# Attention in sub-blocks of 64 positions instead of blocks of 128, ahead of two MLPs

## The chip, the cores and the metric

The kernel runs on one core of a Trainium2 chip. The metric is the device time of one execution in microseconds (us). The times before are 577.37 us (median of three runs, 576.85 to 577.47).

## The reference

A gated linear attention runs over 4 sequences of 768 positions with 8 heads; its output goes through two MLPs of width 256 to 2048 to 256. The attention is written in chunks of 32 positions, but its result does not depend on the chunk: a kernel may take any length, as long as it hands the state on.

```python
for c in range(nc):
    cum = np.cumsum(la, axis=-1)
    L = np.exp(cum[:, :, :, None] - cum[:, :, None, :]) * causal
    M = np.einsum('bhin,bhjn->bhij', Cc, Bc) * L
    y_intra = np.einsum('bhij,bhjd->bhid', M, xc)
    y_inter = np.einsum('bhin,bhnd->bhid', Cc, state) * np.exp(cum)[:, :, :, None]
    y[:, :, sl] = y_intra + y_inter
    Bx = np.einsum('bhjn,bhjd->bhjnd', Bc, xc) * decay_from_j[:, :, :, None, None]
    state = decay_full[:, :, None, None] * state + np.sum(Bx, axis=2)
x = softplus(x @ w_in) @ w_out              # first MLP
g = np.where(h >= 1, h, np.where(h <= -1, 0, (h + 1) ** 2 / 4))   # second MLP, h = x @ w2_in
return g @ w2_out
```

## The kernel before

The 768 positions are cut into six blocks (c = 0 to 5) of Q = 128. A unit u is one block of one sequence, so there are 24 units; from the second block on, two sequences of a block are worked on as a pair. The first MLP takes a block's 512 columns as soon as its four units are done, and its matmuls fill TensorE between the attention's.

`program()` lists the work as jobs with an engine, a cost, what they need and which buffers they take. A planner (`Jobs.order`) turns the list into one fixed order for each engine, and `tile_kernel` emits it. So a changed cost or need moves instructions far from the code that changed. Each engine works its list strictly in order; a job that waits holds back all that stands behind it.

For a pair from the second block on, the jobs are: `rows` (a transfer that copies a unit's clipped decays to all 128 partitions), `decay` (one VectorE scan a unit, L915, that turns them into the matrix of decays, 128 positions by 8 heads by 128), `scores` (TensorE, L951, the products of C and B), `weigh` (VectorE, L960, scores times decays, two a unit), `cd` (L935, C times the running decay), `sources` (L923, B times the decay to the block's end), and `out` (TensorE): the part from the old state (L986), the part within the block (L993), and in the same PSUM tile the block's own sum for the next state (L1000; not in the last block). Then `evac` copies the output from PSUM (ScalarE, L1019), `ready` subtracts for its low half (VectorE, L1027) and updates the state (L1030), and `sm` spreads the state for the next block's `out` (ScalarE, L1038). There is one pair of PSUM banks, `y`, which `scores` and `out` share in turn; `ready` gives it back.

These matmuls have plain 32-bit operands; each is recorded as two passes, and each pass as a weight load and a matmul. They use a part of the array each (32 or 128 rows by 32, 64 or 128 columns), and those on different parts run side by side. The MLP's matmuls (L1061 to L1063, L1197) use the whole array.

Of the kernel before, what the change touches and what calls it, by code (L numbers as in the profile page):

```python
# [15 lines left out]
Q = 128  # L16
NC = S // Q
NU = NC * NB
# [171 lines left out]

def ready_of(u):

    return u if u < NB else u | 1
# [7 lines left out]
def program():  # L201
# [39 lines left out]
    for u in range(NU):  # L241
# [4 lines left out]
        if c == 0:  # L246
            for hg in range(2):
                add(
                    ("spread", u, hg), PE, 470, needs=[("columns", hg), ("rows_of", u)] + ([("spread", u, 0)] if hg else []),
                    takes=[("acc", "h")] + ["ld"] * (hg == 0),  # L250
                )
                add(("decay", u, hg), ACT, 520, needs=[("spread", u, hg)], gives=[("part", ("spread", u, hg), 0)])
            decay = [("decay", u, 0), ("decay", u, 1)]
        else:
            add(("rows", u), SP, 400, needs=["store"], takes=["ld"], size=524e3)
            add(("decay", u), DVE, 2220, needs=[("rows", u)])
            decay = [("decay", u)]
            add(("cd", u), DVE, 200, needs=[("load", u), ("dec", c)])
# [6 lines left out]
        elif c < NC - 1:  # L265
            add(("sources", u), DVE, 210, needs=[("load", u)] + decay, takes=["bt"])
        if b % 2:
            v = u // 2
            add(
                ("scores", v), PE, 1270, needs=[("load_bc", v)] + (decay + [("decay", u - 1)] if c else [("scores", v - 1)] * v),  # L270
# [3 lines left out]
        for hg in range(2):  # L274
            n = 2 * u + hg
            weighed = [("decay", u, hg), ("sources", u, hg)] if c == 0 else decay + [("sources", u)] * (c < NC - 1)
# [6 lines left out]
            else:  # L283
                add(("weigh", u, hg), DVE, 600, needs=weighed + [("weigh", u, 0)] * hg + [("scores", u // 2)], gives=bank)
        both = [u] if c == 0 else [u - 1, u]
        if c == 0 or b % 2:

            needs = [("weigh", i, hg) for i in both for hg in range(2)] + ([("out", both[0] - 1)] if u else [])
            if c > 0:
                needs += [(kind, i - NB * (kind == "sm")) for i in both for kind in ("cd", "sm")]  # L290
            add(
                ("out", u), PE, 2200 if c else 750, needs=needs, takes=["y"],
                gives=[("load", i) for i in both] + [("rows", i) if c else ("part", ("spread", u, 0), 1) for i in both]
                + [("sources", i) if c else ("sources", u, 0) for i in both] * (c < NC - 1),
# [5 lines left out]
            if c == 1:  # L300
# [5 lines left out]
                ("ready", u), DVE, 610 + 380 * (c < NC - 1) if c else 340, due=due, needs=[("evac", u)],  # L306
                gives=[("out", u)] + [("dec", c)] * (b == NB - 1 and c > 0),
            )
        if c < NC - 1:
            add(("sm", u), ACT, 500, needs=[("ready", ready_of(u))] + [("decay", 3, 1)] * (u < NB))  # L310
# [165 lines left out]
DEC_DMAS = 1  # L476
# [10 lines left out]
def tile_kernel(ctx: ExitStack, tc: tile.TileContext, a0, al, bc, ub, w_in, w_out, w2_in, w2_out, out):  # L487
# [48 lines left out]
    s_t = [base.tile([128, 64], F32, name=f"s{b}") for b in range(NB - 1)]  # L536
# [5 lines left out]
    base.tile([128, 244], F32, name="pad")  # L542
# [6 lines left out]
    eye_t = base.tile([128, H * Q], F32, tag="eye0", name="eye_t")  # L549
    sm_t = [base.tile([128, 64], F32, name=f"sm{b}") for b in range(NB)]  # L550
    s_t.append(base.tile([128, 64], F32, name="s3"))
    idle, eye16, later = (base.tile([128, Q], BF16, name=n) for n in ("idle", "eye16", "later"))

    more = [base.tile([128, 512], F32, tag=f"more{i}", name=f"more{i}") for i in range(1)]
# [6 lines left out]
    def home(tag):  # L561

        if tag not in homes:
            n = {"ld": 1024, "st": 1024, "eye": 1024, "bc": 768}.get(tag[:-1], 512)
# [7 lines left out]
    units = [(f"u{i}", 0) for i in range(4)] + [("eye0", 0), ("eye0", 1), ("dec0", 0), ("dec1", 0), ("more0", 0)]  # L572
# [7 lines left out]
    def plain(tag, part):  # L580

        key = tag + " plain"
        if key not in homes:
            n = {"st": 1024, "eye": 1024}.get(tag[:-1], 512)
# [20 lines left out]
    clip_z = dram.tile([NU, H * Q], F32, name="clip_z")  # L605
    clip_p = dram.tile([NC * 2, 4, NB, Q], F32, name="clip_p")
# [178 lines left out]
    heads, z_t = (flat(buf("dec", i)).rearrange("p (h i) -> p h i", h=4)[0:nr] for i in range(2))  # L785
# [51 lines left out]
    @job  # L837
    def clip_load(engine):
        tiles["clip"] = new(of("clip_load"), F32, "clip0").rearrange("p (h i) -> p h i", h=4)[0:nr]
        nc.sync.dma_start(tiles["clip"], al.rearrange("r (h i) -> r h i", h=4))  # L840
# [9 lines left out]
    def store(engine, *step):  # L850
# [5 lines left out]
        else:  # L856
            nc.sync.dma_start(clip_z.rearrange("u (g h i) -> (u g) h i", g=2, i=Q), z_t)
# [30 lines left out]
    def rows(engine, u):  # L888
# [3 lines left out]
        nc.sync.dma_start(flat(ld_t(u)), clip_z[r:r + 1].to_broadcast([128, H * Q]))  # L892

    @job
    def dec(engine, c):
        t = mine("dec", c)[0]
        src = clip_p.rearrange("(c g) h b i -> c (g h) (b i)", g=2)[c]
        nc.sync.dma_start(flat(t), src.unsqueeze(1).to_broadcast([H, N, NB * Q]))

    def ld_t(u):  # L900
        return buf(*got["rows", u][0]) if u >= NB else buf(*got["spread", u, 0][1])
# [18 lines left out]
    def sources(engine, u, hg=None):  # L920
# [4 lines left out]
            in1=ld_t(u)[:, h, Q - 1:Q].to_broadcast([128, h.stop - h.start, N]), op=ALU.mult,  # L925
# [6 lines left out]
    def cd(engine, u):  # L932

        t = parts(u)[2]
        nc.vector.tensor_tensor(out=t, in0=t, in1=mine("dec", u // NB)[0][:, u % NB, :], op=ALU.mult)  # L935
# [21 lines left out]
    def weigh(engine, u, hg):  # L957
        ld = flat(ld_t(u)[:, 4 * hg:4 * hg + 4])
        if engine == DVE:
            nc.vector.tensor_tensor(out=ld, in0=cb_t(u, hg), in1=ld, op=ALU.mult)  # L960
# [14 lines left out]

    def out_unit(engine, u):
        c, b = divmod(u, NB)
        units = [u] if c == 0 else [u - 1, u]

        if c > 0:  # L980
            for i in units:
                y, cdt = y_t(i)[0], parts(i)[2]
                for p in range(4):

                    r, o = slice(p * 32, p * 32 + 32), p % 2 * 64
                    nc.tensor.matmul(  # L986
                        y[o:o + 64, p // 2], sm_t[i % NB][r], cdt[r], start=(i == units[0]), stop=False, skip_group_check=True,
                    )
        for i in units:
            y, x, ld = y_t(i)[0], parts(i)[0], ld_t(i)  # L990
            for h in range(H):
                r = slice(h % 4 * 32, h % 4 * 32 + 32)
                nc.tensor.matmul(  # L993
                    y[r, h // 4], x[:, h * 32:h * 32 + 32], ld[:, h, :], start=(c == 0), stop=True, skip_group_check=True,
                )
        for i in units if c < NC - 1 else []:
            state, x, bt = y_t(i)[1], parts(i)[0], flat(bt_t(i))
            for p in range(4):
# [4 lines left out]
                )  # L1003

# [9 lines left out]
    def evac(engine, u):  # L1014
# [5 lines left out]
        if c == 0:  # L1020
            nc.scalar.copy(s_t[b], y_t(u)[1])

    @job
    def ready(engine, u):
# [3 lines left out]
        for i in (u - 1, u) if 0 < c < NC - 1 else ():  # L1028
            s = s_t[i % NB]
            nc.vector.scalar_tensor_tensor(  # L1030
                out=s, in0=s, scalar=mine("dec", c)[0][:, i % NB, Q - 1:Q], in1=y_t(i)[1], op0=ALU.mult, op1=ALU.add,
            )

    @job
    def sm(engine, u):
        b = u % NB
        for e in range(2):
            nc.scalar.activation(  # L1038
                out=sm_t[b][:, e * D:(e + 1) * D], in_=s_t[b][:, e * D:(e + 1) * D], func=AF.Copy, scale=of_one[:, e:e + 1],
            )  # L1040
# [183 lines left out]
    with tc.manual_schedule():  # L1224
# [3 lines left out]
        for i in range(WARM):  # L1228
# [4 lines left out]
        ones = buf("ld", 4)  # L1233
        nc.gpsimd.memset(ones[:, 0:2], 1.0)
        eye3 = eye_t.rearrange("p (h i) -> p h i", h=H)
        nc.gpsimd.affine_select(
            out=eye3[:, 0], in_=ones[:, 0], pattern=[[1, Q]],
# [8 lines left out]
        nc.vector.tensor_copy(eye16, eye3[:, 0])  # L1246
# [78 lines left out]
```

## Time and profile before

| | before |
|---|---|
| median of three runs | 577.37 us |
| profiled execution: time, span | 577.67 us, 576.0 us |
| TensorE busy | 563.8 us (98%) |
| VectorE busy | 461.2 us (80%) |
| ScalarE busy | 340.8 us (59%) |
| matmul passes | 3526 |

Busy times overlap, so they don't add up to the span. A matmul's recorded duration is longer than the time by which it holds up the next one: matmuls are pipelined, and what counts is the distance between their starts. The time that is not in the span (577.67 - 576.0 = 1.67 us) lies around it.

### The profile page before, as it was taken

How to read it: one execution, taken by the hardware profiler on the slowest of the kernel's cores; microseconds unless marked ns; L12 is line 12 of the kernel's file. 1: busy time of each engine (PE TensorE's matmuls, PEld its weight loads, DVE VectorE, ACT ScalarE, POOL GpSimd, SP SyncE). 2: the span in 40 equal slices, each digit the busy share in tenths (PEclk: the TensorE clock that was granted, in tenths of full speed). 3: DMA queues.
4: the chain of work that ended last, by engine and by line, in shares of the span. 5: the costliest groups of instructions: out<-in, count | busy, mean ns of one | idle time of the engine just before them, and what ended most of it. 6: DMA issues, size and time to landing. Idle time of an engine off the chain costs nothing.

```text
span 576.0 us, 9160 instructions
## 1 busy us (share of the span) xinstructions
PE 563.8 (98%) x3526; PEld 468.8 (81%) x3526; DVE 461.2 (80%) x777; ACT 340.8 (59%) x615; POOL 42.9 (7%) x42
## 2 busy tenths in 40 slices
PE   7799999999999999999999999999999999999997
PEld 3699989998877877888888788888887888788885
DVE  6899999968756684589999888987799776776674
ACT  5858554424414512666456777766677674777863
POOL 5211300000000340010000000200021000000000
PEclk9999999999999999999999999999999999999999
DMA  7976245514303200023431000000100001000001
GB/s 276 399 275 225 81 160 199 164 63 138 129 22 116 75 1 1 0 75 92 128 116 67 1 1 1 1 0 2 73 2 1 1 1 38 36 1 1 1 1 73
DMA packets 19863, 43.67 MB, mean 76 GB/s; under 512 B 1740, under 2 KB 2316, under 8 KB 19820
## 3 DMA queue, kind: packets, MB, share of 16 engines
q1 hardware_dynamic: 19820, 43.10, 22.0%
q8 instruction: 27, 0.44, 0.3%
q14 instruction: 16, 0.13, 0.1%
HBM read 39.75 MB, written 3.34 MB: 75 GB/s over the span
## 4 chain that ended last, share of the span: by engine, by line
PE 91%; DVE 5%; DMA 1%; issue 1%; ACT 1%; SPq 0%; DVEq 0%
PE acc L1197 42%; PE h L1061 6%; PE h L1063 6%; PE h L1062 6%; PE h L1068 3%; PE h L1070 3%; PE h L1069 3%; PE z L1068 3%; PE z L1070 3%; PE z L1069 3%; PE acc L1185 2%; PE y L951 2%; PE y L993 2%; PE z L1063 1%; PE z L1061 1%; PE z L1062 1%
## 5 line engine op out<-in xcount | busy, mean ns | idle before, releaser
L1171 DVE TENSOR_TENSOR gl<-g,gh 128x512 fp32r<-128x512 f32 x182 | 128.1, 706 | 36.3 <-PE acc L1197 22.2
L1197 PE MATMUL acc<-gh,woh 128*128 128x512 f32 (+1 forms) x424 | 152.3, 367 | 0.0
L1197 PE MATMUL acc<-gh,wol 128*128 128x512 f32 (+1 forms) x424 | 150.6, 363 | 0.0
L1197 PE MATMUL acc<-gl,woh 128*128 128x512 f32 (+1 forms) x424 | 115.5, 363 | 0.0
L1156 ACT ACTIVATE g<-h 128x512 f32<-128x512 f32 x74 | 44.2, 597 | 96.0 <-PE h L1063 88.9
L1197 PEld LDWEIGHTS acc<-gh,woh 128*128 128x128 f32 x424 | 79.8, 188 | 15.8 <-issue 1.7
L1197 PEld LDWEIGHTS acc<-gh,wol 128*128 128x128 f32 x424 | 79.9, 189 | 12.3
L611 ACT CAST gh<-g 128x512 fp32r<-128x512 f32 x110 | 68.2, 620 | 33.2 <-PE acc L1197 22.2
L1197 PEld LDWEIGHTS acc<-gl,woh 128*128 128x128 f32 x424 | 74.4, 189 | 12.7
L1061 PE MATMUL h<-xh,wih 128*128 128x256 f32 (+1 forms) x224 | 74.9, 334 | 0.0
L1062 PE MATMUL h<-xh,wil 128*128 128x256 f32 (+1 forms) x224 | 73.6, 328 | 0.0
L1063 PE MATMUL h<-xl,wih 128*128 128x256 f32 (+1 forms) x224 | 73.6, 328 | 0.0
L1148 ACT ACTIVATE t<-t 128x512 f32<-128x512 f32 x96 | 60.9, 634 | 2.2
L613 DVE CAST gh<-g 128x512 fp32r<-128x512 f32 x76 | 35.2, 467 | 26.6 <-ACT g L1156 22.4
L915 DVE TENSOR_TENSOR_SCAN ld<-ld,eye_t 128x1024 f32<-128x1024 f32 x20 | 47.3, 2367 | 1.9 <-DMA ld<-clip_z 1.9
L1061 PEld LDWEIGHTS h<-xh,wih 128*128 128x128 f32 x224 | 42.6, 190 | 4.6 <-issue 0.7
L1063 PEld LDWEIGHTS h<-xl,wih 128*128 128x128 f32 x224 | 42.5, 190 | 3.8
L1062 PEld LDWEIGHTS h<-xh,wil 128*128 128x128 f32 x224 | 42.6, 190 | 3.8
L1141 ACT ACTIVATE t<-h 128x512 f32<-128x512 f32 x37 | 22.1, 597 | 14.8 <-PE h L1070 11.5
L1141 ACT ACTIVATE t<-z 128x512 f32<-128x512 f32 x35 | 20.8, 595 | 9.7 <-PE z L1070 7.7
L1160 DVE TENSOR_TENSOR g<-h,t 128x512 f32<-128x512 f32 x37 | 25.4, 686 | 0.9 <-ACT t L1148 0.2
L1160 DVE TENSOR_TENSOR g<-z,t 128x512 f32<-128x512 f32 x35 | 23.9, 685 | 0.6
(335 smaller groups left out, 900.1 us busy)
## 6 DMA issues: line engine op xcount, KB each, us to landing
ld<-clip_z SPq DMA_DIRECT2D x20, 512.0 KB, 4.4
st<-in_w_in_dram SPq DMA_DIRECT2D x15, 512.0 KB, 4.0
st<-in_w_out_dram SPq DMA_DIRECT2D x15, 512.0 KB, 4.6
u<-in_ub_dram SPq DMA_DIRECT2D x24, 256.0 KB, 4.8
bc<-in_bc_dram SPq DMA_DIRECT2D x12, 384.0 KB, 6.1
out_dram<-st_plain SPq DMA_DIRECT2D x6, 256.0 KB, 2.2
dec<-clip_p SPq DMA_DIRECT2D x5, 256.0 KB
out_dram<-dec_plain SPq DMA_DIRECT2D x4, 256.0 KB
```

Source lines behind the costliest of these rows:

```text
L611: nc.scalar.copy(out, in_)
L613: engines[engine].tensor_copy(out, in_)
L915: nc.vector.tensor_tensor_scan(t, t, eye_t, 0.0, ALU.mult, ALU.add)
L1061: nc.tensor.matmul(o, wh, xh[c][:, k, t0:t0 + n], start=(k == 0), stop=False)
L1062: nc.tensor.matmul(o, wl, xh[c][:, k, t0:t0 + n], start=False, stop=False)
L1063: nc.tensor.matmul(o, wh, xl[c][:, k, t0:t0 + n], start=False, stop=(k == 1))
L1141: nc.scalar.activation(out=t, in_=ph, func=act_funcs.IDENTITY_SAT240, scale=SAT)
L1148: nc.scalar.activation(out=t, in_=t, func=AF.Square, scale=0.5 / SAT, bias=0.5)
L1156: nc.scalar.activation(out=g, in_=ph, func=AF.Softplus)
L1160: nc.vector.tensor_tensor(out=g, in0=ph, in1=t, op=ALU.max)
L1171: engines[engine].tensor_tensor(out=mine("g_lo", s)[0], in0=mine("g", s)[0], in1=mine("g_hi", s)[0].bitcast(F32), op=ALU.subtract)
L1197: nc.tensor.matmul(acc_t(s, e), w, g[:, j * n:(j + 1) * n], start=(begins(e, j) and g is gh and i == 0), stop=(fc + j == NFC - 1 and g is ...
```

## The change

From the second block on, a block of 128 is worked on as two sub-blocks of 64. The decays of a unit are now 128 partitions (two sub-blocks of 64 positions) by 8 heads by 64, half as many numbers as before. `rows` copies each sub-block with a transfer of its own, `dec` likewise; both units of a pair share one buffer. `scores` makes 16 smaller matmuls instead of 8, within the block 32 instead of 16, from the old state 16 instead of 8, for the new state 16 instead of 8. Since the second sub-block needs the state after the first, `out` is split: a new job `st` makes half of the part within the sub-blocks and both sub-blocks' sums, a new job `carry` (VectorE) updates the state by the first sub-block, `sm(u, 1)` (ScalarE) spreads it, and only then `out` adds the part from both states and the other half. `st` and `sources` are now also in the last block. The buffer `y` is held from `st` to `ready`. The first block is as before, except for the shapes of some small tiles.

```diff
+HALF = 64
...
-            add(("rows", u), SP, 400, needs=["store"], takes=["ld"], size=524e3)
-            add(("decay", u), DVE, 2220, needs=[("rows", u)])
+            add(("rows", u), SP, 800, needs=["store"] + [("rows", u - 1)] * (b % 2), takes=["ld"] * (b % 2 == 0), size=262e3)
+            add(("decay", u), DVE, 1130, needs=[("rows", u)])
...
             if c > 0:
-                needs += [(kind, i - NB * (kind == "sm")) for i in both for kind in ("cd", "sm")]
+                add(
+                    ("st", u), PE, 850, needs=needs + [("sm", u - NB)], takes=["y"], gives=[("sources", i) for i in both],
+                )
+                add(("carry", u), DVE, 300, needs=[("st", u), ("dec", c)])
+                add(("sm", u, 1), ACT, 500, needs=[("carry", u)])
+                needs = [("st", u), ("sm", u, 1)] + [("cd", i) for i in both]
...
-        nc.sync.dma_start(flat(ld_t(u)), clip_z[r:r + 1].to_broadcast([128, H * Q]))
+        for s in range(2):
+            nc.sync.dma_start(flat(ld_t(u)[s * HALF:(s + 1) * HALF]), clip_z[r, s:s + 1].to_broadcast([HALF, H * HALF]))
...
+                if 2 * v >= NB:
+                    for s in range(2):
+                        o = slice(HALF * s, HALF * s + HALF)
+                        nc.tensor.matmul(
+                            cb_t(2 * v + q // 2, q % 2)[o, p * 128:(p + 1) * 128], t[r, p * 128 + s * HALF:][:, :HALF],
+                            t[r, 256 + p * 256 + s * 128:][:, :128], start=True, stop=True,
+                        )
+                    continue
...
+    def st(engine, u):
+
+        intra_turn(u, 0)
+        for i in range(2):
+            x, bt = parts(u - 1 + i)[0], flat(bt_t(u - 1 + i))
+            for p in range(4):
+                for s in range(2):
+                    r, o = slice(s * HALF, s * HALF + HALF), slice(p * 32, p * 32 + 32)
+                    nc.tensor.matmul(
+                        states_t(u, s)[o, i], bt[r, p * 32:p * 32 + 32], x[r, p * 64:p * 64 + 64], start=False, stop=True,
+                        skip_group_check=True,
+                    )
...
+    def carry_on(u, s):
+
+        c, b = divmod(u, NB)
+        for i in range(2):
+            state = s_t[b // 2][:, i]
+            nc.vector.scalar_tensor_tensor(
+                out=state, in0=state, scalar=dec_t(c)[:, s, b - 1 + i, HALF - 1:HALF], in1=states_t(u, s)[:, i],
+                op0=ALU.mult, op1=ALU.add,
+            )
...
+    def intra(i, h, o, r, start):
+        y, x, ld = y_t(i)[0], parts(i)[0], ld_t(i)
+        k, col = h // 4, slice(h % 4 * 32, h % 4 * 32 + 32)
+        nc.tensor.matmul(
+            y[col, k, o], x[r, h * 32:h * 32 + 32], ld[r, h, :], start=start, stop=True, skip_group_check=True,
+        )
...
+        for i in (u - 1, u):
+            for h in range(4):
+                for s in range(2):
+                    intra(i, (s + turn) % 2 * 4 + h, halves[s], halves[s], turn == 0 and i == u - 1)
...
+            for s in range(2):
+                for p in range(4):
+
+                    r, o = slice(p * 32, p * 32 + 32), p % 2 * 64
+                    nc.tensor.matmul(
+                        y[o:o + 64, p // 2, halves[s]], sm_t[b // 2][s][r, i % 2], cdt[r, halves[s]], start=False,
+                        stop=False, skip_group_check=True,
+                    )
+        intra_turn(u, 1)
```

How the instructions stand now is seen best at the first pair of the second block. On TensorE its `out` was one run of matmuls (names: `sm` old state, `ld` decays, `bt` sources, `u` inputs, `gh`, `gl`, `woh`, `wol` operands of the MLP; "x8" is eight matmuls):

```order
L1197 MATMUL acc_240<-gl,woh_98 128x256 x4
L986 MATMUL y<-u_131,sm_142 64x128 x4
L986 MATMUL y<-u_132,sm_143 64x128 x4
L993 MATMUL y<-ld_123,u_131 32x128 x8
L993 MATMUL y<-ld_119,u_132 32x128 x8
L1000 MATMUL y<-u_131,bt_260 32x64 x4
L1000 MATMUL y<-u_132,bt_296 32x64 x4
```

Now `st` stands first, TensorE, same place (L1037 is the part within a sub-block, L1015 the sums for the state):

```order
L1263 MATMUL acc_217<-gl,woh_94 128x256 x4
L1037 MATMUL y<-ld_121,u_129 32x64 x8
L1037 MATMUL y<-ld_121,u_130 32x64 x8
L1015 MATMUL y<-u_129,bt_259 32x64 x8
L1015 MATMUL y<-u_130,bt_295 32x64 x8
```

After 24 matmuls of 256 columns of the MLP the rest follows (L1069 is the part from the two states, `sm_140` and `sm_141`); then come 12 matmuls of the MLP, and the next pair's `scores` (L972):

```order
L1263 MATMUL acc_217<-gl,woh_95 128x256 x4
L1069 MATMUL y<-u_129,sm_140 64x64 x4
L1069 MATMUL y<-u_129,sm_141 64x64 x4
L1069 MATMUL y<-u_130,sm_140 64x64 x4
L1069 MATMUL y<-u_130,sm_141 64x64 x4
L1037 MATMUL y<-ld_121,u_129 32x64 x8
L1037 MATMUL y<-ld_121,u_130 32x64 x8
```

So a run of 64 passes became two runs of 64 passes, with MLP matmuls between them: 24 of 256 columns or 12 of 512 at all ten pairs (one has 12 and 6).

On VectorE at the same pair the two scans of the next pair stood one behind the other, and `ready` (L1027, L1030) behind them (the listing prints a scan as SCALAR_TENSOR_TENSOR):

```order
L915 SCALAR_TENSOR_TENSOR ld_120<-ld_120,eye_t 128x1024
L1219 TENSOR_TENSOR xl_308<-acc_240,xh_307 128x256
L915 SCALAR_TENSOR_TENSOR ld_121<-ld_121,eye_t 128x1024
L1219 TENSOR_TENSOR xl_308<-acc_240,xh_307 128x256
L1027 TENSOR_TENSOR xl_984<-y,xh_983 128x2x256
L1030 SCALAR_TENSOR_TENSOR s_66<-s_66,dec_135,y 128x64
```

Now VectorE has (L933 the scan of half the length, L1025 first `carry`, at the end the update in `ready`, L1097 its subtraction):

```order
L933 SCALAR_TENSOR_TENSOR ld_117<-ld_117,eye_t 128x512
L1025 SCALAR_TENSOR_TENSOR s_66<-s_66,dec_133,y 128x64 x2
L933 SCALAR_TENSOR_TENSOR ld_117<-ld_117,eye_t 128x512
L941 TENSOR_TENSOR bt_251<-u_131,ld_117 128x128
L941 TENSOR_TENSOR bt_259<-u_132,ld_117 128x128
L933 SCALAR_TENSOR_TENSOR ld_118<-ld_118,eye_t 128x512
L1237 TENSOR_TENSOR gl<-g,gh 128x512
L1097 TENSOR_TENSOR xl_1041<-y,xh_1040 128x2x256
L1025 SCALAR_TENSOR_TENSOR s_66<-s_66,dec_133,y 128x64 x2
```

So `carry` stands directly behind one scan, and `ready` behind two further scans and a subtraction of the MLP.

## Rows read from the trace of the kernel before

**Rows 1.** The page: busy time of the engines; the chain that ended last.

```profile
PE 563.8 (98%) x3526; PEld 468.8 (81%) x3526; DVE 461.2 (80%) x777; ACT 340.8 (59%) x615; POOL 42.9 (7%) x42
...
PE 91%; DVE 5%; DMA 1%; issue 1%; ACT 1%; SPq 0%; DVEq 0%
```

**Rows 2.** TensorE's waits: line, releaser, us in total, times, longest.

```profile
PE z L1068 <- DVE z L1111: 1.3, 2, 0.9
...
PE y L951 <- DVE s L1030: 0.4, 1, 0.4
```

**Rows 3.** Timeline of TensorE at one pair's `scores`: start us, us, instruction.

```profile
82.48 0.28 PE L1063 MATMUL h<-xl,wih 128*128 128x256 f32 x1
82.69 0.48 PE L951 MATMUL y<-bc 32*128 32x256 f32 x2
82.70 0.48 PE L951 MATMUL acc<-bc 32*128 32x256 f32 x2
...
83.44 0.38 PE L951 MATMUL y<-bc 32*128 32x256 f32 x2
...
83.77 0.38 PE L1197 MATMUL acc<-gh,woh 128*128 128x256 f32 x1
83.99 0.28 PE L1197 MATMUL acc<-gh,wol 128*128 128x256 f32 x1
```

**Rows 4.** Timeline of TensorE at one pair's `out`.

```profile
86.50 0.28 PE L1062 MATMUL h<-xh,wil 128*128 128x256 f32 x1
86.62 0.28 PE L1063 MATMUL h<-xl,wih 128*128 128x256 f32 x1
86.83 0.67 PE L986 MATMUL y<-u,sm 32*64 32x128 f32 x16
87.43 1.08 PE L993 MATMUL y<-ld,u 128*32 128x128 f32 x32
88.32 0.41 PE L1000 MATMUL y<-u,bt 128*32 128x64 f32 x16
88.66 0.38 PE L1197 MATMUL acc<-gh,woh 128*128 128x256 f32 x1
88.88 0.28 PE L1197 MATMUL acc<-gh,wol 128*128 128x256 f32 x1
```

**Rows 5.** The same for a pair of the last block.

```profile
217.74 0.61 PE L1197 MATMUL acc<-gl,woh 128*128 128x512 f32 x2
...
218.88 1.08 PE L993 MATMUL y<-ld,u 128*32 128x128 f32 x32
219.89 0.50 PE L1197 MATMUL acc<-gh,woh 128*128 128x512 f32 x1
```

**Rows 6.** L986: duration ns min/median/max, first and last start; PEldq is the sequencer.

```profile
L986 PE MATMUL y<-u,sm x160: 267/268/318, 68.9 to 232.7; 32*64 32x128 f32 x160
L986 PEldq EVENT_SEMAPHORE  x10: 51/51/51, 66.6 to 228.0; - x10
```

**Rows 7.** L1000, columns as before.

```profile
L1000 PE MATMUL y<-u,bt x160: 219/219/219, 13.3 to 194.8; 128*32 128x64 f32 x160
```

**Rows 8.** Groups of VectorE by line and shape: count, busy us, mean ns, idle before.

```profile
L915 DVE TENSOR_TENSOR_SCAN ld<-ld,eye_t 128x1024 f32<-128x1024 f32 x20 | 47.3, 2367 | 1.9 <-DMA ld<-clip_z 1.9
...
L960 DVE TENSOR_TENSOR ld<-acc,ld 128x512 f32<-128x512 f32 x24 | 16.3, 681 | 0.1
```

**Rows 9.** Timeline of all engines behind another pair's `out`.

```profile
176.33 0.41 PE L1000 MATMUL y<-u,bt 128*32 128x64 f32 x16
...
176.81 0.59 ACT L1019 CAST xh<-y 128x512 fp32r<-128x512 f32 x1 [2.57 <-PE y L1000]
...
177.43 0.69 DVE L1027 TENSOR_TENSOR xl<-y,xh 128x512 fp32r<-128x512 f32 x1 [0.33 <-ACT xh L1019]
178.04 0.46 DVE L1030 SCALAR_TENSOR_TENSOR s<-s,dec,y 128x64 f32<-128x64 f32 x2
...
178.92 0.95 ACT L1038 ACTIVATE sm<-s,of_one 128x32 f32<-128x32 f32 x4
```

More of the change, by code (lines that the diff above doesn't have):

```diff
@@ L283, in program @@
             else:
[L284 removed]
+                add(("weigh", u, hg), DVE, 340 if c else 600, needs=weighed + [("weigh", u, 0)] * hg + [("scores", u // 2)], gives=bank)
         both = [u] if c == 0 else [u - 1, u]
@@ L289, in program @@
             if c > 0:
-                needs += [(kind, i - NB * (kind == "sm")) for i in both for kind in ("cd", "sm")]
-            add(
-                ("out", u), PE, 2200 if c else 750, needs=needs, takes=["y"],
-                gives=[("load", i) for i in both] + [("rows", i) if c else ("part", ("spread", u, 0), 1) for i in both]
-                + [("sources", i) if c else ("sources", u, 0) for i in both] * (c < NC - 1),
+                add(
[4 more added lines that the diff above has]
+                needs = [("st", u), ("sm", u, 1)] + [("cd", i) for i in both]
+            add(
+                ("out", u), PE, 750 if c else 750, needs=needs, takes=["y"] * (c == 0),
+                gives=[("load", i) for i in both] + [("rows", u - 1) if c else ("part", ("spread", u, 0), 1)]
+                + [("sources", u, 0)] * (c == 0),
             )
@@ L305, in program @@
             add(
-                ("ready", u), DVE, 610 + 380 * (c < NC - 1) if c else 340, due=due, needs=[("evac", u)],
-                gives=[("out", u)] + [("dec", c)] * (b == NB - 1 and c > 0),
-            )
-        if c < NC - 1:
-            add(("sm", u), ACT, 500, needs=[("ready", ready_of(u))] + [("decay", 3, 1)] * (u < NB))
+                ("ready", u), DVE, 610 + 300 * (c < NC - 1) if c else 340, due=due, needs=[("evac", u)],
+                gives=[("st", u) if c else ("out", u)] + [("dec", c)] * (b == NB - 1 and c > 0),
+            )
+        if c < NC - 1 and b % 2:
+            add(("sm", u), ACT, 500, needs=[("ready", i) for i in ((u - 1, u) if c == 0 else (u,))] + [("decay", 3, 1)] * (u < NB))
     last_use, first_use = {}, {}
@@ new lines, in carry_on, with carry @@
+    def carry_on(u, s):
[6 more added lines that the diff above has]
+            )
+    @job
+    def carry(engine, u):
+        carry_on(u, 0)
+    def intra(i, h, o, r, start):
[4 more added lines that the diff above has]
+        )
@@ L976, in out_unit, with intra_turn @@
+    halves = [slice(s * HALF, s * HALF + HALF) for s in range(2)]
+    def intra_turn(u, turn):
+        for i in (u - 1, u):
+            for h in range(4):
+                for s in range(2):
+                    intra(i, (s + turn) % 2 * 4 + h, halves[s], halves[s], turn == 0 and i == u - 1)
     def out_unit(engine, u):
         c, b = divmod(u, NB)
[L978 to L988, printed above, removed]
@@ L989, in out_unit @@
-        for i in units:
-            y, x, ld = y_t(i)[0], parts(i)[0], ld_t(i)
-            for h in range(H):
[L992 to L997, printed above, removed]
+        if c == 0:
+            for h in range(H):
+                intra(u, h, slice(0, Q), slice(0, Q), True)
+            state, x, bt = y_t(u)[1], parts(u)[0], flat(bt_t(u))
@@ L1003, in out_unit @@
                 )
+            return
+        for i in (u - 1, u):
+            y, cdt = y_t(i)[0], parts(i)[2]
+            for s in range(2):
+                for p in range(4):
[3 more added lines that the diff above has]
+                        stop=False, skip_group_check=True,
+                    )
+        intra_turn(u, 1)
     emit["out"] = out_unit
```

101 lines of the change are left out of this document (55 added, 46 removed).

## Prediction

> **What bounds the kernel.** I read the engines' busy times first: TensorE is busy 98% of the span, and the chain that ended last runs over TensorE for 91%, over VectorE for 5% [rows 1]. A busy TensorE need not be a full one, so next come its waits: behind the start there are only small ones, of which the attention's is 0.4 us, a `scores` that waited for the state update on VectorE to give `y` back, and the longest group is 1.3 us in the second MLP [rows 2]. So TensorE works one dense list, and what the change is worth is the change in the time for which the attention's matmuls hold that list up. VectorE saves much (below), but little waits for it.
>
> That time is read from starts. **`scores`**: the last MLP matmul starts at 82.48 and holds the engine for 0.12 (the distance of two such matmuls, 86.50 to 86.62), so it is free at 82.60. The first passes start at 82.69, four within 0.02 us, so four parts of the array work side by side; the next MLP matmul starts at 83.77, and the one behind it 0.22 later instead of 0.12 [rows 3, 4]. In all 83.77 - 82.60 + 0.10 = 1.27 us. **`out`**: free at 86.74, MLP again at 88.66, again 0.10 late: 2.02 us [rows 4]. In the last block, without the sums for the state: 217.74 plus two matmuls of 0.227 is 218.19, to 219.89, 1.70 + 0.10 = 1.80 us [rows 5]. A pair costs 3.29 us (eight pairs) or 3.07 (two).
>
> **Prices for the new shapes.** Passes go in batches of four. L993 has 32 passes, 8 batches of 128 columns, in 88.32 - 87.43 = 0.89: 0.11 a batch. L1000 has 4 batches of 64 columns; its last pass starts 0.41 - 0.22 = 0.19 after the first, less 0.02 for its place in the batch: three distances of 0.055 [rows 4, 7]. L986, 4 batches of 128 columns with weights 64 wide, takes 87.43 - 86.83 = 0.60 with the change to the next shape [rows 4]: 0.44 for the batches, the rest for the first weights (0.05) and the change (0.11). Going in from the MLP costs 0.09 (82.60 to 82.69). Leaving L1000: 88.51 (the last start) to 88.66, less its batch: 0.095.
>
> **The change on TensorE.** Eight passes side by side, which no row shows, is the unknown. From above: batches of eight take the time of a batch of four. From below: two batches of four. I take the first, since rows show four side by side in rows (L951), in columns (L993) and in both (L986), and eight starts at the spacing of L951 (four in 0.02) fit into 0.055. Then, for a pair:
> - `scores`: 32 passes, 4 batches of 128 columns, 64 wide: like L986, 0.09 + 0.60, and 0.03 for eight starts: 0.72.
> - `st`: 64 passes, 8 batches of 64 columns: 0.09 + 0.02 (first weights) + 0.44 + 0.03 + 0.095 = 0.68.
> - `out`: the states' part is 32 passes in 8 batches of four (its four parts already fill the array's rows) of 64 columns with weights 64 wide. Between 0.055 (L1000, narrow weights) and 0.11 (L986, twice the columns) I take 0.065, near the first: 0.52. With 0.09 in, 0.05 first weights, 0.11 change of shape, 4 batches of 0.055, 0.02 and 0.03, and 0.095 out: 1.13.
> - Three returns to the MLP instead of two: 0.30.
>
> The sum is 2.83 us: 0.46 less than 3.29, and 0.24 less than 3.07 in the last block, where `st` and its sums are new work. 8 x 0.46 + 2 x 0.24 = 4.2 us saved. If every batch stays at four, `scores` is 1.16, `st` 1.12 and `out` 1.35, with returns 3.93: 0.64 and 0.86 more, 6.8 us lost.
>
> **What the change adds as waits.** `out` now waits for `st`, `carry`, `sm`. From rows behind another `out`: ScalarE starts 0.07 after the last matmul's end (176.74 to 176.81), the two state updates take 0.46, two activations of `sm` about 0.5 (four take 0.95), and between the engines 0.1 to 0.4: 1.1 to 1.5 us [rows 9]. In between TensorE has 24 MLP matmuls of 0.12 or 12 of 0.227, 2.7 to 2.9 us: hidden, with 1.2 us to spare. `carry` stands behind one scan (now half of 2.37, about 1.2) [rows 8]; if that scan starts just ahead, the spare is just used up. What is queued behind `carry` are scans and `ready`, behind the waiting `out` the MLP. The other wait is for `y`: at the first pair of the second block 12 matmuls, 1.44 us, stand between `out` and the next `scores`, while `evac`, `ready` and its state update take 0.07 + 0.59 + 0.62 + 0.46 = 1.75 [rows 9]: about 0.4 late, the size of the wait that is there now [rows 2], so no change. Elsewhere 2.9 us or more stand there. For chance hits over the first eight pairs, where two scans and a subtraction (0.69) can stand ahead of `ready`, I add 0.5.
>
> **Edits that cost nothing.** VectorE saves about 20 x 1.2 for the scans and 40 x 0.3 for `weigh` (0.68 each, half the columns) [rows 8], and pays ten `carry` of 0.46 and four `sources`; TensorE's list hides all of it, and if it did not, VectorE would still have less to do than before. ScalarE's `sm` are as many as before. The transfers are twice as many and half the bytes; scans waited 1.9 us for them in the whole run [rows 8], and none of that reached TensorE [rows 2]. On SP the rows of each pair's second unit now stand behind the store of the running products in the second block; the same small wait for transfers is the cover, and if it went, the scans behind would be late and with them `scores`.
>
> Sum: -4.2 + 0.5 = -3.7 on the profiled 577.67, 574.0; the median is 0.3 lower than that execution, so **573.6 us**.
>
> **The rivals.**
> *Passes can't be fed so fast (slower).* An `out` now issues 64 passes from 86.83 to 88.51, 26 ns a pass, the fastest long run in the trace [rows 4]. The sequencer runs ahead: it passes the wait of the first `out` at 66.6, and TensorE starts it at 68.9; 2.3 us at 0.12 are 19 passes [rows 6]. If 26 ns were the limit behind those 19, `st` and `out` would each take 45 x 0.026 + 0.25 = 1.42, `scores` stays, and a pair is 0.72 + 2.84 + 0.30 = 3.86: 0.57 and 0.79 more, 6.1 us, **584** with the 0.5. It decides from about 20 ns a pass (45 x 2 x 0.020 eats the 0.46). Against it: in L1000 passes start 0.19/15 = 13 ns apart, for 16 passes [rows 4, 7]; for it: no row shows a longer run as fast.
>
> [...]
>
> *Four side by side at most (slower).* 6.8 lost and 0.5: **585**. The price is above; rows for more than four are missing.
>
> *Waits take the gain (no change).* If `out` or `scores` comes 0.4 us late at each pair, the time is **577.5**. Speaks for it: two scans ahead of `ready`. Against it: in the second and third block VectorE is relieved by about 3 us a pair.
>
> *States' batches at 0.11 (no change).* 8 x 0.045 more a pair, 3.6 us: **577.2**.
>
> *VectorE's relief reaches further (faster).* Were the 1.3 us of waits in the second MLP to go too [rows 2], **572.3**. Those waits are of sums made long after the last scan, so I give it little.
>
> **How the numbers follow.** 0.2% of 577 us, 1.15 us, is about what a measurement of this kernel can tell from no change. Forecast 0.60, further relief 0.07, waits 0.08, slow batches of states 0.06, feeding 0.13, four at most 0.06. So faster 0.68 (the forecast and the relief, less a little), same 0.13, slower 0.19. The forecast's own range is 570 to 576; the range reaches from 569.5 to 581, for feeding between 20 and 26 ns, and leaves out the two slow ends.
>
> **What would show it.** Right: runs of `scores`, `st` and `out` of 0.7, 0.7 and 1.1 us between MLP matmuls, eight starts within about 0.05 us; no wait of TensorE for ScalarE's `sm` above some tenths. Wrong: starts in `st` spaced evenly at 20 ns or more from some pass on (feeding), or batches of four at 0.055 (no eight side by side), or an idle TensorE ahead of L1069 or L972.

## The result: slower by 0.9%, where 0.7% faster was predicted

The changed kernel takes 582.36 us (median of four runs, 581.21 to 583.92) against 577.26 (576.85 to 577.47); the ratio is 1.0091, with a 95% interval of 1.0064 to 1.0118. The profiled execution took 583.0 us with a span of 581.3, 5.3 more than before. In both profiled executions the granted clock of TensorE is 1.00 in every stretch up to the last matmul, so the clock isn't what differs.

The page of the changed kernel, where it answers to [rows 1]: busy times, and the chain that ended last.

```profile
PE 564.0 (97%) x4358; PEld 467.2 (80%) x4358; DVE 443.1 (76%) x812; ACT 337.6 (58%) x608; POOL 34.1 (6%) x39
...
PE 87%; DMA 4%; DVE 3%; ACT 3%; issue 1%; SPq 1%; DVEq 0%; ACTq 0%
```

VectorE is relieved by 18 us, but transfers are now 4% of the chain, against 1%. First TensorE, one pair's `scores` (start us, us, instruction), which answers to [rows 3]:

```profile
67.22 0.64 PE L1263 MATMUL acc<-gl,woh 128*128 128x256 f32 x4
67.79 0.34 PE L972 MATMUL y<-bc 32*64 32x128 f32 x4
...
68.19 0.29 PE L972 MATMUL acc<-bc 32*64 32x128 f32 x4
68.41 0.38 PE L1263 MATMUL acc<-gh,woh 128*128 128x256 f32 x1
```

and another pair's `st` and `out`, for [rows 4]:

```profile
149.74 0.61 PE L1263 MATMUL acc<-gl,woh 128*128 128x512 f32 x2
150.28 0.47 PE L1037 MATMUL y<-ld,u 64*32 64x64 f32 x32
150.55 0.59 PE L1015 MATMUL y<-u,bt 64*32 64x64 f32 x32
151.07 0.50 PE L1263 MATMUL acc<-gh,woh 128*128 128x512 f32 x1
...
153.70 0.39 PE L1129 MATMUL h<-xl,wih 128*128 128x512 f32 x1
154.02 0.69 PE L1069 MATMUL y<-u,sm 32*64 32x64 f32 x32
154.64 0.45 PE L1037 MATMUL y<-ld,u 64*32 64x64 f32 x32
155.03 0.50 PE L1263 MATMUL acc<-gh,woh 128*128 128x512 f32 x1
```

Read as before, `scores` holds TensorE for 68.41 - 67.70 = 0.71 us, `st` for 151.07 - 150.19 = 0.88 (0.97 at four other pairs), `out` for 155.03 - 153.93 = 1.10, each without the 0.10 of the return. Over the whole run the attention holds it for 37.95 us instead of 41.00 (the sum of such differences): 3.05 saved. The loss is elsewhere. The idle time between MLP matmuls (each distance beyond the usual 0.12 or 0.227, summed) rose from 14.8 to 22.5 us: 4.4 of the 7.7 before 60 us, 2.0 from 60 to 85, 1.0 from 85 to 240 (the third return of each pair), 0.3 later. With -3.05 that makes 4.65; the rest of the 5.3 is the tail behind the last matmul, 4.6 us instead of 4.0. The new waits, for [rows 2]:

```profile
PE acc L1263 <- DVE wol L778: 1.9, 2, 1.7
...
PE h L1127 <- ACT g L1222: 1.4, 2, 0.7
...
PE acc L1263 <- DVE gl L1237: 1.3, 1, 1.3
```

L778 makes the low half of a weight of the first MLP. VectorE and ScalarE, which convert the weights, waited for their transfers in turn (engine, line, releaser: us, times, longest; between 15 and 75 us):

```profile
ACT t L691 <- DMA st<-in_w_out_dram: 4.4, 2, 2.6
ACT t L691 <- DMA ld<-clip_z: 3.8, 1, 3.8
ACT t L691 <- DMA st<-in_w_in_dram: 2.9, 2, 2.2
```

```profile
DVE w L679 <- DMA st<-in_w_out_dram: 3.0, 1, 3.0
DVE w L679 <- DMA st<-in_w_in_dram: 2.6, 1, 2.6
```

The four rows that name weights (`st`) make 12.9 us, against 0.3 in the kernel before. The 3.8 us put to rows (`ld`) are of the same kind: L691 reads only weights, and its sequencer passed its wait for `st` at 46.34, 0.05 us before L691 started. With them it is 16.7. TensorE's share of it is seen in one stretch, 45 to 60 us (stretch, its length, busy us of each engine, clock, share of the DMA engines, GB/s), first of the kernel before, then of the changed one:

```profile
45.00:60.00 15.00, 15.00 (x133) 14.51 (x132) 14.10 (x25) 13.65 (x24) 3.29 (x2) 1.00 0.62 198
```

```profile
45.00:60.00 15.00, 10.87 (x84) 10.06 (x84) 8.87 (x17) 6.53 (x11) 0.00 (x0) 1.00 0.97 256
```

What is ahead of the weights shows on SP's queue (start us, us, instruction; `st` are weights, `ld` rows, `clip_p` the store of the running products), before:

```profile
23.48 1.42 SPq L892 DMA_DIRECT2D ld<-clip_z  x3
25.00 0.38 SPq L658 DMA_DIRECT2D st<-in_w_in_dram  x1
25.43 1.57 SPq L892 DMA_DIRECT2D ld<-clip_z  x2
32.34 0.38 SPq L658 DMA_DIRECT2D st<-in_w_out_dram  x1
35.75 0.38 SPq L658 DMA_DIRECT2D st<-in_w_in_dram  x1
37.65 3.29 SPq L871 DMA_DIRECT2D clip_p<-clip  x4
41.05 0.44 SPq L658 DMA_DIRECT2D st<-in_w_out_dram  x1
```

and after:

```profile
28.25 5.64 SPq L902 DMA_DIRECT2D ld<-clip_z  x6
34.00 0.52 SPq L667 DMA_DIRECT2D st<-in_w_out_dram  x1
35.92 3.33 SPq L880 DMA_DIRECT2D clip_p<-clip  x4
39.30 2.44 SPq L902 DMA_DIRECT2D ld<-clip_z  x4
41.85 0.52 SPq L667 DMA_DIRECT2D st<-in_w_in_dram  x1
42.42 2.38 SPq L902 DMA_DIRECT2D ld<-clip_z  x4
44.91 0.52 SPq L667 DMA_DIRECT2D st<-in_w_out_dram  x1
```

A pair now shares a buffer, so the five buffers hold ten units' rows, and the planner fetches all ten before 47 us. The bytes are the same as before (10 x 256 KB for 5 x 512), but the transfers are 20 instead of 5, half of them among the weights; the weights of 35.75 us went out at 41.85. Between 28 and 36 us the DMA engines moved 227 GB/s instead of 368, though they were nearly as busy (a share of 0.92 against 1.01).

### The profile page after: what moved, and what is told of

The parts are those of the page before. It is cut to its first block, busy times and chain, and to the rows that moved or that the text cites. A ratio compares the mean times of both kernels' runs of the same rounds, so it can differ in the third digit from the quotient of the medians.

```text
span 581.3 us, 10861 instructions
## 1 busy us (share of the span) xinstructions
PE 564.0 (97%) x4358; PEld 467.2 (80%) x4358; DVE 443.1 (76%) x812; ACT 337.6 (58%) x608; POOL 34.1 (6%) x39
## 4 chain that ended last, share of the span: by engine, by line
PE 87%; DMA 4%; DVE 3%; ACT 3%; issue 1%; SPq 1%; DVEq 0%; ACTq 0%
PE acc L1263 42%; PE h L1127 6%; PE h L1128 6%; PE h L1129 6%; PE h L1134 3%; PE h L1136 3%; PE z L1134 3%; PE h L1135 3%; PE z L1136 3%; PE z L1135 3%; DMA st<-in_w_out_dram 3%; PE acc L1251 2%; PE y L1037 1%; PE z L1129 1%; PE z L1128 1%; PE z L1127 1%
## 5 line engine op out<-in xcount | busy, mean ns | idle before, releaser
L620 ACT CAST gh<-g 128x512 fp32r<-128x512 f32 x102 | 63.2, 620 | 31.3 <-PE acc L1263 20.2
L1127 PE MATMUL h<-xh,wih 128*128 128x256 f32 (+1 forms) x224 | 76.3, 341 | 1.4 <-ACT g L1222 1.4
L622 DVE CAST gh<-g 128x512 fp32r<-128x512 f32 x84 | 39.8, 476 | 45.7 <-ACT g L1222 41.4
L1207 ACT ACTIVATE t<-h 128x512 f32<-128x512 f32 x37 | 22.1, 598 | 14.8 <-PE h L1136 11.5
L933 DVE TENSOR_TENSOR_SCAN ld<-ld,eye_t 128x512 f32<-128x512 f32 x20 | 23.9, 1212 | 0.3 <-DMA ld<-clip_z 0.2
```

What stands on the lines that cost most here:

```text
L620: nc.scalar.copy(out, in_)
L622: engines[engine].tensor_copy(out, in_)
L1127: nc.tensor.matmul(o, wh, xh[c][:, k, t0:t0 + n], start=(k == 0), stop=False)
L1207: nc.scalar.activation(out=t, in_=ph, func=act_funcs.IDENTITY_SAT240, scale=SAT)
```

## The experiments

Times are medians with the ratio to the kernel before on the same chip and its interval. Three explanations stood against each other: the number of transfers on SP (the expectations call it the queue or number theory), their slow packets (packet or partition theory), and their place ahead of the weights; a rival was the new order on TensorE and VectorE (order theory). Durations of packets are from the trace's records of the DMA engines; averages of 4 KB packets are over 20 to 42 us. That a transfer on SP waits for the eighth one before it, as the expectations say, shows in the changed kernel: the transfers of 28.25, 29.42 and 31.38 us were issued when those of 21.38, 22.11 and 22.55, each eight places ahead, had landed, at 28.23, 29.41 and 31.37. In the traces of halves, copies and fast_rows TensorE's granted clock stood at 0.5 for 3.4 us before 64 us, in that of two_queues for 6.8 us (on average it was 0.89 over 45 to 60 us of halves and over 15 to 30 us of fast_rows, and 0.995 and 0.993 over the whole of copies and two_queues). Their medians don't rest on it: at a mean granted clock of 0.999 or more they took 582.5, 582.3, 579.0 to 579.4 and 580.9 to 581.1 us.

**one, one_late.** One transfer a unit, from two rows, each to 64 partitions:

```diff
-        for s in range(2):
-            nc.sync.dma_start(flat(ld_t(u)[s * HALF:(s + 1) * HALF]), clip_z[r, s:s + 1].to_broadcast([HALF, H * HALF]))
+        src = clip_z[r].unsqueeze(1)
+        nc.sync.dma_start(flat(ld_t(u)), src.to_broadcast([2, HALF, H * HALF]))
```

> The changed kernel, in which each unit's rows are copied by one transfer to 128 partitions instead of two to 64; the bytes, the packets' size and the order on every engine stay. Queue theory (the weights of the first MLP come late because 20 transfers stand among them on SP, each taking 0.45 to 0.6 us to issue, and because a transfer waits until the eighth one before it has landed): the ten issues saved give back 5 to 6 us of SP's time before 47 us, so TensorE's new gaps between 51 and 70 us (5.2 us in all) shrink to 1 to 2 us and the time is 578 to 579.5. Packet theory (packets of 2 KB keep the DMA engines busy without moving much): the packets stay, so the gaps stay, 581.5 to 582.5. Order theory (the planner's new order on TensorE and VectorE makes the gaps): 582.

639.11 us, 1.1064 (1.1043 to 1.1085). The transfers view of 20 to 70 us:

```profile
GB/s 402 392 387 390 385 342 133 59 48 220 233 48 49 49 49 49 48 49 49 49 49 49 49 252 223 71 66 49 49 49 44 50 51 128 297 75 49 49 49 49
```

The rows moved at 49 GB/s, with the DMA engines busy for 0.13 of the time (38 to 45 us), as if two of the 16 worked (0.13 x 16 = 2.1); the source of this form has an outer dimension of two. That says nothing on the theories, except that the form of such a transfer matters.

> Both edits: one transfer a unit, and the same 12 units' worth (six units) of rows behind the weight loads. Queue theory: four transfers ahead of the weights, like the kernel before; the gaps are gone and the time is that of the run with late rows or up to 0.7 us less, 574 to 575.5. Packet theory: as the run with late rows, 574.5 to 576. Order theory: 582.

626.52, 1.0849 (1.0828 to 1.0871): the same.

**late.** Only SP's list is altered; units 8 to 13 are in truth both pairs of the third block and the first of the fourth (the expectation names them wrongly):

```diff
-        for name, engine, slots in order:
+        last, behind = 0.0, {8: ("load_w", 1, "i", 1), 10: ("load_bc", 5)}
+        for name, engine, slots in moved(order, {("rows", u): behind[min(u & ~1, 10)] for u in range(8, 14)}):
...
+moved = lambda order, to: [j for i in order if i[0] not in to for j in [i] + [k for k in order if to.get(k[0]) == i[0]]]
```

> The changed kernel with its two transfers a unit, in which only SP's order is altered: the rows of the third pair of the second block and of the two pairs of the third block (12 of the 20 early transfers) stand behind weight loads of 55 us and later instead of ahead of those of 34 us and later. Queue theory: eight transfers of rows are left ahead of the weights, against five in the kernel before; the gaps between 51 and 70 us fall below 1 us, and with 3.0 us saved in the attention and 1.0 us of added returns and waits the time is 574.5 to 576. Packet theory: the same, since the bytes go too. Order theory: TensorE's and VectorE's orders are unchanged, so 582.

577.53, 0.9991 (0.9971 to 1.0011): 5 us are back without any other engine's list being touched, so the order theory falls. The stretch of 45 to 60 us of this run:

```profile
45.00:60.00 15.00, 15.00 (x127) 15.00 (x127) 14.63 (x24) 12.48 (x22) 1.29 (x1) 1.00 0.77 228
```

Its queue on SP, where the weights follow each other now:

```profile
33.57 3.34 SPq L880 DMA_DIRECT2D clip_p<-clip  x4
36.95 2.44 SPq L902 DMA_DIRECT2D ld<-clip_z  x4
39.51 0.52 SPq L667 DMA_DIRECT2D st<-in_w_in_dram  x1
40.15 0.39 SPq L667 DMA_DIRECT2D st<-in_w_out_dram  x1
```

TensorE is full again, the waits for weights are 4.5 us instead of 12.9, TensorE's idle time is 15.8 instead of 22.5. The median is 1.5 us above what was expected. The executions spread from 575.96 to 580.02 us, which isn't explained; the profiled one has a span of 574.3, 1.7 below the kernel before.

**split, split_columns, split_even, split4, split3.** The kernel before, its rows cut into more transfers:

```diff
-        nc.sync.dma_start(flat(ld_t(u)), clip_z[r:r + 1].to_broadcast([128, H * Q]))
+        for s in (0, 64): nc.sync.dma_start(flat(ld_t(u)[s:s + 64]), clip_z[r:r + 1].to_broadcast([64, H * Q]))
```

(split_columns: two halves of the columns to all partitions; split_even: `ld_t(u)[s::2]` for s in 0, 1; split4: four times 32 partitions; split3: 0 to 31, 32 to 95, 96 to 127.)

> The kernel before (128 positions, nothing else changed), each unit's rows by two transfers to 64 partitions. Queue theory: five more issues of 0.45 to 0.6 us before 30 us, where SP then waits 5 us for a free staging buffer, so SP has room; what is left is that the weight load behind them may wait for the eighth transfer before it: 0 to 1.5 us lost, 577.3 to 578.8. Packet theory: packets stay at 4 KB, 577.3. Order theory: 577.3. If this alone lost 3 us or more, the transfers' number would be the whole story without the larger prefetch.

579.83, 1.0024 (1.0007 to 1.0041): the 4 KB packets became slow (266 ns on average instead of 170), which none of the three had foreseen.

> The kernel before, each unit's rows by two transfers as in the run split, but cut by columns: each goes to all 128 partitions with 512 of the 1024 columns (packets of 2 KB). Number theory (each further transfer costs SP 0.45 to 0.6 us, and only eight are in flight): as many transfers as in split, so the same loss, 579 to 580.5. Partition theory (a transfer into 64 partitions alone has slow packets: in split a 4 KB packet took 265 ns on average between 25 and 38 us, against 170 in the kernel before): packets of 2 KB at about 84 to 91 ns, the weights as early as before, 577 to 577.8.

577.57, 0.9999 (0.9990 to 1.0008): as many transfers, no loss. The number theory falls here. 28 to 36 us of the two runs, split first:

```profile
28.00:36.00 8.00, 8.00 (x57) 7.58 (x55) 7.59 (x13) 4.80 (x8) 4.26 (x2) 1.00 1.04 260
```

```profile
28.00:36.00 8.00, 8.00 (x51) 7.42 (x50) 7.71 (x13) 4.53 (x8) 2.67 (x2) 1.00 1.04 360
```

Equally busy DMA engines move 260 GB/s or 360.

> The kernel before, each unit's rows by two transfers to 64 partitions as in split, but to the even and to the odd partitions. If packets are slow because they go to one half of the partitions at a time: 4 KB packets at 159 to 175 ns as in the kernel before, 577.3. If they are slow because a transfer has 64 packets instead of 128, whatever the place: 4 KB packets at about 265 ns and 579 to 580.5, as split.

577.93, 1.0010 (0.9992 to 1.0028); 4 KB packets 170 ns on average, as in the kernel before (170; 266 in split): not 64 partitions are slow, but 64 neighbouring ones.

> The kernel before, each unit's rows by four transfers to 32 neighbouring partitions each. If a packet slows down with the number of neighbouring partitions that a transfer fills (128: 170 ns, 64: 265 ns): about 450 to 550 ns for 4 KB, and 4 to 10 us lost. If 64 and 32 are alike (the cost is that of any split by partition): about 265 ns and 579 to 582.

578.31, 1.0014 (1.0002 to 1.0025), 4 KB packets 258 ns: 32 neighbouring partitions are no slower than 64. The time is below the expected 579 to 582.

> The kernel before, each unit's rows by three transfers, to partitions 0 to 31, 32 to 95 and 96 to 127. [...] If a transfer to 64 neighbouring partitions is slow wherever it lies, nearly all take 240 to 280, as in split and split4. The time is 577.5 to 579 either way.

577.59, 0.9997 (0.9983 to 1.0011); 4 KB packets 252 ns, and 22% of them took up to 170 ns, against 8% in split and 23% in split4 (258 ns): about as slow as in split4, not "nearly all" of them slow; inconclusive.

**halves, late_halves.** The changed kernel, both units of a pair in one transfer for each sub-block (10 early transfers to 64 partitions instead of 20, all at the first unit's place):

```diff
+        t, src = flat(buf(*got["rows", u & ~1][0])).rearrange("p (u i) -> p u i", u=2), clip_z[r:min(r + NC + 1, NU):NC]
+        for s in range(2 - u % 2 * 2): nc.sync.dma_start(t[s * HALF:(s + 1) * HALF], src[:, s].unsqueeze(0).to_broadcast([HALF, 2, H * HALF]))
```

> The changed kernel with one transfer for a pair's first sub-blocks and one for its second: 10 early transfers to 64 partitions instead of 20, each with two packets of 2 KB a partition, the same bytes, all issued at the place of the pair's first unit. Number theory: SP gets back ten issues, 5.5 us, between 39 and 47 us; the weights there come 3 to 5 us earlier and the time falls to 578 to 579.5. Partition theory: 2.6 MB go into half of the partitions at a time at some 235 GB/s, 11 us, and the weight loads of 26 to 40 us stand behind them: 581 to 583, no gain.

582.16, 1.0079 (1.0059 to 1.0098): half the transfers, no gain.

> The edits of the runs late and halves together: two transfers a pair, three of the five early pairs behind the weight loads. Number theory: four transfers of rows are left ahead of the weights instead of eight, 2.4 us less on SP between 37 and 40 us: 0 to 1 us below the run late, 575 to 577. Partition theory: as late, 576 to 577.6. Either way TensorE's gaps between 51 and 70 us stay below 1 us in all.

577.09, 0.9999 (0.9985 to 1.0014), as late.

**two_queues.** `nc.gpsimd` issues the second sub-block's transfer.

> The changed kernel, the second sub-block's transfer of each unit issued by GpSimd instead of SP. Number theory: SP issues ten transfers less before 47 us, the time falls to 578 to 579.5, and packets last as long as before (2 KB between 24 and 34 us: 116 ns on average). Partition theory: the two queues' packets go to both halves of the partitions in turn, so a 2 KB packet takes 84 to 95 ns, and the time falls to 576 to 578. If GpSimd's issues are late, scans on VectorE wait for them instead and the time is over 580.

581.33, 1.0064 (1.0050 to 1.0079). SP has ten issues less, the 2 KB packets stay slow (119 ns on average on SP's queue between 20 and 60 us). The expectation that the queues would serve both halves at once fails, and so does the number theory's. The third, late issues by GpSimd, fits the time but not the wait: scans waited 1.5 us for rows.

**copies, copies_late, form16.** The clipped decays are stored eight times, and one transfer a unit reads 16 rows for 8 partitions each; form16 uses that form in the kernel before.

```diff
-    clip_z = dram.tile([NU, 2, H * HALF], F32, name="clip_z")
+    clip_z = dram.tile([NU, 2, 8, H * HALF], F32, name="clip_z")
...
+        src = clip_z[r].rearrange("s k i -> (s k) i").unsqueeze(1)
+        nc.sync.dma_start(flat(ld_t(u)), src.to_broadcast([16, 8, H * HALF]))
```

> The changed kernel with the clipped decays stored eight times over, so that one transfer, whose source has 16 rows, each read for 8 partitions, copies a unit's rows to all 128 partitions; 10 early transfers of 256 KB, orders unchanged. Partition theory: 2 KB packets fall from 116 ns to 84 to 92, the DMA moves some 380 GB/s again instead of 235, the weights come as early as in the kernel before, TensorE's gaps between 51 and 70 us fall below 1 us, and the time is 574.5 to 576.5 (3.0 us saved in the attention, 1.0 lost in returns and waits). The store is eight times as large (0.8 MB, about 2 us of the DMA engines near 12 us); if that delays the first loads, up to 1 us of it is lost again. If something other than the rows' transfers makes the weights late, 581 to 583.

582.52, 1.0082 (1.0055 to 1.0109): no gain. Between 29 and 32.5 us 2 KB packets took 144 ns on average, against 134 in the changed kernel, so they are as slow as there, though the form fills all 128 partitions.

> The kernel before, in which the rows' transfer reads 16 rows, each for 8 partitions, instead of one row for 128 (it reads the first 16 units' rows whatever the unit, so the decays are other than the reference's; bytes, partitions and packets stay). If this form makes packets slow, as the run copies suggests (2 KB: 111 ns on average): 4 KB packets at 220 to 280 ns instead of 170, and the time 1 to 3 us above the kernel before. If the form is harmless: 159 to 175 ns and 577.3, and the slow packets of copies come from something else.

578.47, 1.0023 (1.0003 to 1.0043); 4 KB packets 264 ns: this form makes packets slow in the kernel before, too.

> The same, and three of the five early pairs' rows behind the weight loads as in the run late. Partition theory: with fast packets the place of the rows matters little: within 0.7 us of the run copies, and 0.5 to 2 us below the run late (577.5), so 575 to 576.5.

576.16, 0.9966 (0.9951 to 0.9980): the only run that is clearly faster than the kernel before. It is 6.4 us below copies, so the expectation that the place matters little fails. Why it gains more than late isn't shown: its trace is of an execution of 578.3 us, the longest of twelve.

**fast_rows, fast_early, fast_late.** One transfer of one row to 128 partitions (`clip_z[r, 0:1].to_broadcast([128, H * HALF])`), at three places.

> The changed kernel with one transfer a unit of a single 2 KB row to all 128 partitions, the form of the kernel before with half the columns; the second sub-block so gets the first one's decays (a part of the data is other than the reference's, the work on every engine is the same). If slow packets of the rows make the weights late: packets at 84 to 92 ns on average between 22 and 36 us, TensorE's gaps between 51 and 70 us below 1 us, and 574.5 to 576.5. If the bytes or the place of the rows on SP make them late whatever the form, as the run copies could mean: 580 to 582.5.

579.32, 1.0038 (1.0020 to 1.0055): 3 of 5 us are back, which lies between the two expectations. Not all packets became fast: between 22 and 36 us half of them took 84 ns, but the average is 108, against 111 in the changed kernel and in copies. Between 28 and 36 us 257 GB/s were moved, against 256 in copies, which gained nothing. So the average rate doesn't tell why this form is better.

> The run fast_rows (one transfer of one row to 128 partitions a unit; the second sub-block gets the first one's decays), with both units' transfers at the place of the pair's first unit, ahead of the store of the running products, as all early rows stand in the kernel before. If the place among the weights (second units between 38 and 44 us) is what fast_rows still lost: waits of VectorE and ScalarE for weights fall from 9.8 us to 2 to 5 us, and 576 to 577.5. If the place ahead of the weights is as bad (as halves against the changed kernel says for slow packets): 579 to 580.

578.66, 1.0012 (0.9992 to 1.0032), between the two expectations and not clearly apart from fast_rows; waits for weights 6.2 us.

> The run fast_rows with three of the five early pairs' rows behind the weight loads: nothing of the transfers is left to disturb the weights. What stays is the attention's gain (3.3 us in the runs late and after) less about 1.0 us of added returns and waits: 574.8 to 576. If late and copies_late lose something that is no matter of the weights, it stays here too: 576.2 to 577.5.

576.95, 0.9990 (0.9973 to 1.0008), no different from late, and in the second range: something that is no matter of the rows' form is lost here too. What it is stays open.

**priced.** The planner is told dearer rows (`SP, 1200`, `size=370e3`).

> The changed kernel, its planner told what the rows cost by the trace: 1200 ns of SP a unit instead of 800, and 1.4 times the bytes (235 GB/s against its 330). It then puts one weight load each ahead of one more pair of transfers. If the planner's wrong price is the reason that the rows stand ahead of the weights: 576 to 578. If the planner, which gives SP whatever can start first, puts them there at any price: 580.5 to 582.5.

578.37, 1.0013 (0.9998 to 1.0029), and waits for weights of 4.1 us. The lists of all engines changed with it, so this doesn't separate SP's order from theirs; but prices nearer to the trace gave back most of the loss, close to the first of the two expectations.

## Why the prediction was wrong

**The failed step** is in "Edits that cost nothing": "the transfers are twice as many and half the bytes; scans waited 1.9 us for them in the whole run". It asked who waits for the rows. Hardly anyone does (scans waited 0.2 us for them in the changed kernel). It did not ask what stands behind the rows on SP's queue, although it noted the second units' new place behind the store. The weights of the first MLP stand there. They were issued late (one at 41.85 instead of 35.75 us) and behind transfers that kept the DMA engines busy; VectorE and ScalarE waited at least 12.9 us for them, and TensorE lost some 6.4 us before 85 us. Shown is that the place of the rows decides: with three pairs' rows behind the weights the loss is gone in every form but that of the run one (late 0.9991, late_halves 0.9999, copies_late 0.9966, fast_late 0.9990). With the rows left ahead of the weights, the form changes what it costs: two transfers to 64 partitions 1.0091 (halves 1.0079, copies 1.0082), one row to 128 partitions 1.0038, and 1.0012 ahead of the store. How the form acts there isn't shown, since copies and fast_rows moved as many bytes a second. In the kernel before, where only five units' rows go ahead, slow packets alone cost some 0 to 0.2% (split 1.0024, form16 1.0023, split4 1.0014, split3 0.9997). The number of transfers and SP's issue time are not the cause (split_columns 0.9999, halves 1.0079, two_queues 1.0064).

**Why the packets are slow** is not settled. Slow were 4 KB packets to 64 or 32 neighbouring partitions (split 266 ns, split4 258) and from 16 rows to blocks of 8 (form16 264); fast were those to 128 partitions from one row (170 in the kernel before) and to 64 alternate ones (split_even 170). So it is neither the number of partitions that a transfer fills nor the number of transfers (split and split_even have both alike); and neighbouring partitions alone don't tell it, since form16 fills all 128. What in the hardware makes these forms slow, no run shows. split3 (252 ns, 22% of the packets up to 170) tells nothing further, and the slow packets of fast_rows (108 ns on average, half of them 84) stay open. Over all 16 DMA engines 260 GB/s were moved between 28 and 36 us with two transfers to neighbouring halves of the partitions (split), against 368 with one to 128 (the kernel before), and issuing the halves from two queues gave no clear gain (two_queues 1.0064, against 1.0091 from one).

**TensorE.** `scores` was forecast at 0.72 and took 0.71, `out` 1.13 and 1.10, which bears out the batches of eight side by side and the states' batches at 0.065. `st` was mis-sized: 0.68 forecast, 0.88 to 0.97 measured. The sum had no change of shape between its two parts, and the 32 passes of L1015 take 0.375 from first to last start instead of 0.25. Why four pairs take 0.09 more than the others isn't explained. With the 0.10 of three returns a pair costs 2.99 to 3.08 us, not 2.83: about 2.0 us saved instead of 4.2 (3.05 less ten returns). So without the late weights the forecast would still have been some 2 us too low; the runs without the late weights, 1.5 us faster (copies_late) to no faster (late_halves), fit a gain of that size or less, and the profiled execution of late (1.7 us) fits it best. That they differ isn't explained.

**The rivals.** Feeding fell: eight passes start within 0.05 us (150.285 to 150.332), the 64 of `st` within 0.64 (0.74 at four pairs) and the 64 of `out` within 0.86, 10 to 12 and 14 ns apart, below the 20 ns from which this rival would have decided. So over 64 passes on different parts of the array, too, the starts stayed about as close as the 13 ns of L1000. Four at most fell as well. Waits for `sm` did not come; the one for `y` ahead of L972 is 0.3 us, as the 0.4 forecast. VectorE's relief reached nothing further: the 1.3 us for `z` is still there. The loss came by none of the rivals; the slower ones named TensorE. (One slip in the chances: forecast and relief make 0.67, so "less a little" can't be 0.68; nothing hangs on it.)

## What to carry to other kernels

A transfer that hardly anyone waits for can still cost what is queued behind it (here scans waited 0.2 us for rows, and with three pairs' rows behind the weights 1.0091 became 0.9991): look at the queue it joins, at what goes out next on it, and who converts that. Where a change lets more be fetched early because buffers became free, a planner that starts whatever can start first, as the one here, can put it ahead of what is urgent; moving six entries of one list was worth as much as the whole loss. A transfer's form can set its rate (260 GB/s in split, 360 in split_columns, at a busy share of 1.04 in both): compare GB/s at equal busy share of the DMA engines, not the bytes.

## What was not expected of the hardware

64 passes to different quarters and halves of the array started within 0.64 us (`st` at 150.285 us of the changed kernel). The rate at which the DMA engines moved data between 28 and 36 us fell from 368 GB/s to 260 (split) and 227 (the changed kernel) when rows went to 64 neighbouring partitions at a time, at a busy share of 0.92 to 1.04; it fell to 49 GB/s with a source whose outer dimension is two (one, 38 to 45 us, at a busy share of 0.13). Two queues for the two halves gave no clear gain (1.0064, against 1.0091 with one).
